# Reordering the hand-over from the forward to the inverse transform in a spectral filter beside a gated MLP

## The chip, the core and the metric

The kernel runs on one core of one Trainium2 chip. The metric is the device time of one execution in microseconds. The core has a matrix engine (TensorE, "PE" in the profile), a vector engine (VectorE, DVE), a scalar engine (ScalarE, ACT), a general engine (GpSimd, POOL) and SyncE (SP), which here only issues DMAs. Each engine works through its own queue in order; the engines meet through semaphores. DMAs are issued from the queues of SP, ACT and POOL.

## The reference

The input `x` is 2048 rows of 512 values in bf16. It is normalised by rows, and two branches are added to it:

```python
xn = layernorm(x)                                   # no scale, no shift
X  = rfft2(xn) * (w_r + 1j * w_i)                   # 2048 x 257 filter
A  = irfft2(X)
g, u = xn @ w_gate, xn @ w_up                       # 512 -> 1792
B  = (gelu(g) * u) @ w_down                         # 1792 -> 512
out = x + A + B
```

## The kernel before

The MLP branch is a steady stream of dense matrix products on TensorE. It goes over the rows in four blocks `b` of 512, and in each block over 14 slices `fc` of the hidden width: `gate(b, fc)` (four matmuls of line 851, a gelu on ScalarE in line 854), `up(b, fc)` (four matmuls of line 866, a multiply on VectorE in line 872), and between them pieces of the down projection (`down`, line 887, or `product`, seven matmuls of line 754).

The spectral branch is cut into small units that are slipped into this stream. The Fourier transforms are matrix products with tables of cosines and sines:

- Forward, in four chunks `m` of rows: `unit_D` (transform along the columns), then `units_A(m)`: two groups `g` of matmuls (lines 472 and 475), each copied out of its two PSUM banks by one instruction into the tile `tt` (line 480), and written to the DRAM scratch `scr1` by two DMAs `ri` of 128 KB (issued by the helper in line 337). `load_tv(m)` reads `scr1` back into the tile `tv`, in another arrangement, by two DMAs of 256 KB.
- Inverse, in eight groups `g`: `unit_B(g)` (matmuls of line 571 on `tv`, a copy in line 577, multiplies with the filter in line 582), `unit_C(g)` (line 596, with the twiddle table `cm`, a copy in line 601, a write to a second scratch), later `unit_E` (line 624) and `unit_F` (line 809). `unit_B(0)` needs all four chunks of `tv`.
- The last spectral column goes its own way in small steps `mini(0)` to `mini(4)`.

The filter comes from DRAM in eight slices, `load_W(s)`: eight DMAs of 64 KB each, four for `w_r` on POOL's queue and four for `w_i` on SP's. Slice `s` is what `unit_B(s)` multiplies with; `keep_256(s)` copies its last column aside on POOL (line 560). The table `cm` comes in four pieces of 192 KB on POOL's queue, each for two of the `unit_C`. Loads of this kind go through `load_late` (line 340), which makes the issue wait for the TensorE instruction that was last put into the program.

The order is written out by hand. After each gate, each up and each product the builder calls `hook()`, which counts up by one and puts into the program whatever `at(h, ...)` has planned for that number:

```python
for s, h0 in enumerate((20, 27, 34, 40, 61, 66, 70, 75)):
    for i, t in enumerate(load_W(s)):
        at(h0 + i // 2, t)
    at(89 + s // 2 if s > 3 else 47 + s, (keep_256, s))
```

`units_A(3)` stands at hook 44, `load_tv(3)` at 47, `unit_B(0)` at 59, `unit_B(1)`, `unit_C(0)` and `mini(1)` at 63, `unit_B(2)` and `unit_C(1)` at 68, `unit_B(3)` at 72, `unit_B(4)` at 77. The hooks 57, 60 and 63 follow a gate, 58, 61 and 64 an up, 59, 62 and 65 a product. PSUM has eight banks; `take(n, ...)` picks the bank, or the pair of banks, which by the planner's own reckoning of time is free first, and the semaphores then hold a matmul until its bank has really been emptied.

Of the kernel before, what the change touches and what calls it, by code (L numbers as in the profile page):

```python
# [7 lines left out]
ACT = mybir.ActivationFunctionType  # L8
ALU = mybir.AluOpType
BF16 = mybir.dt.bfloat16  # L10
F16 = mybir.dt.float16
# [4 lines left out]
KD = 256  # L16
# [8 lines left out]
SC_A = 2.0 ** -3  # L25
# [106 lines left out]
class _Prog:  # L132
# [17 lines left out]
    def op(self, eng, fn, r=(), w=(), dma=False, after=()):  # L150
        deps = [(ev, True) for ev in after]
        for k in r:
            if k in self.writer:
                deps.append((self.writer[k], True))
        for k in w:
            if k in self.writer:
                deps.append((self.writer[k], False))
            for ev in self.readers.get(k, ()):
                deps.append((ev, False))
        need = {}  # L160
        for (st, val), raw in deps:
            if st == eng and not dma and (eng == "pe" or not raw):
                continue
            need[st] = max(need.get(st, 0), val)
        known = self.known[eng]
        need = {s: v for s, v in need.items() if known.get(s, 0) < v}
        need = {s: v for s, v in need.items()
                if not any(s2 != s and self.clk[(s2, v2)].get(s, 0) >= v for s2, v2 in need.items())}
        for s, v in need.items():
            for a, b in self.clk[(s, v)].items():  # L170
                if known.get(a, 0) < b:
                    known[a] = b
        if dma:

            st = None if eng == "pool" else next((d for d in self.dsem if known.get(d, 0) >= self.cnt[d]), None)
            if st is None:
                st = "d%d" % (len(self.sem) - 4)
                self.sem[st] = self.es.enter_context(self.nc.semaphore("s_" + st))
                self.cnt[st] = 0
                if eng != "pool":  # L180
                    self.dsem.append(st)
            self.cnt[st] += 16
            ev, inc = (st, self.cnt[st]), 16
            clk = dict(known)
        else:
            self.cnt[eng] += 1
            ev, inc = (eng, self.cnt[eng]), 1
            clk = dict(self.lastclk[eng])
            for a, b in known.items():
                if clk.get(a, 0) < b:  # L190
                    clk[a] = b
        clk[ev[0]] = ev[1]
        self.clk[ev] = clk
        if not dma:
            self.lastclk[eng] = clk
        self.q[eng].append((fn, list(need.items()), ev[0], inc))
        for k in r:
            self.readers.setdefault(k, []).append(ev)
        for k in w:
            self.writer[k] = ev  # L200
            self.readers[k] = []
        return ev
# [12 lines left out]
def bass_parallel_sum__spectral_gfnet__glu_gated_geglu__prompt_kernel(  # L215
# [15 lines left out]
    c_cm = nc.inline_tensor(CM_np, name="c_cm")  # L231
    c_g = nc.inline_tensor(G_np, name="c_g")
    c_mm = nc.inline_tensor(MM_np, name="c_mm")
    scr1 = nc.dram_tensor("scr1", (64, 64 * KD), F16).ap()
    scr2 = nc.dram_tensor("scr2", (P, 32 * KD), BF16).ap()

    xv = A_x.rearrange("o (q b j) d -> b q (o j) d", b=2, j=NJ)
# [5 lines left out]
    with ExitStack() as es:  # L243
# [4 lines left out]
        op = pr.op  # L248
# [29 lines left out]
        tt = [early[:, 4096 + 1024 * i:5120 + 1024 * i].rearrange("p (b jj c) -> p b jj c", b=2, jj=2) for i in range(4)]  # L278
# [32 lines left out]
        def bank(i):  # L311
            return psum[:, i * 512:(i + 1) * 512]
# [4 lines left out]
        def pair(i):  # L317
            return psum[:, i * 512:(i + 2) * 512]
# [5 lines left out]
        def take(n, dur, hold=None, ops=1):  # L324
            i = min(range(9 - n), key=lambda i: max(free[i:i + n]))
            pt[0] += dur
            if hold is None:
                act_t[0] = max(act_t[0], pt[0] + 0.25) + 0.2 + 0.43 * n
                end = act_t[0]
            else:  # L330
                end = pt[0] + hold
            for k in range(i, i + n):
                free[k] = end
            return i

        def dma(eng, dst, src, r=(), w=()):
            return op(eng, lambda e: e.dma_start(dst, src), r=r, w=w, dma=True)  # L337
# [122 lines left out]
        def units_A(m):  # L460

            for g in range(2):
                bk = take(2, 0.5)
                i = (2 * m + g) % 4

                def fn(e, bk=bk, g=g):
                    ins = None
                    for jj in range(2):
                        j = 4 * m + 2 * g + jj
                        x4 = xs[j % 8]  # L470
                        for b in range(2):
                            e.matmul(bank(bk + b)[:, 256 * jj:256 * jj + 256], am[64 * b:64 * b + 64, j, 64:192], x4[64 * b:64 * b + 64, 0:256],
                                     start=True, stop=False, skip_group_check=True)
                        for b in range(2):
                            ins = e.matmul(bank(bk + b)[:, 256 * jj + 1:256 * jj + 256], am[64 * b:64 * b + 64, j, 0:128], x4[64 * b:64 * b + 64, 256:511],  # L475
                                           start=False, stop=True, skip_group_check=True)
                    return ins

                op("pe", fn, r=["am"] + [("xs", (4 * m + 2 * g + jj) % 8) for jj in range(2)], w=[("ps", bk), ("ps", bk + 1)])
                op("act", lambda e, bk=bk, i=i: e.activation(tt[i].rearrange("p b jj c -> p (b jj c)"), pair(bk), ACT.Copy, scale=SC_A),  # L480
                   r=[("ps", bk), ("ps", bk + 1)], w=[("tt", i)])
                n = 2 * m + g
                for ri in range(2):
                    dma("act" if m == 3 and ri else "sp", scr1[8 * n:8 * n + 8, :].rearrange("(l i) (x c) -> i x l c", i=2, c=KD)[ri],
                        tt[i][64 * ri:64 * ri + 64].rearrange("p b jj c -> p (b jj) c"), r=[("tt", i)], w=[("scr1", n, ri)])

        MA, TA, MB, MC, TC, ME = (mm[:, 0:256], mm[:, 256:320], mm[:, 320:384], mm[:, 384:640], mm[:, 640:704], mm[:, 704:768])
# [61 lines left out]
        def load_W(s):  # L549
            hs = slice(2 * s, 2 * s + 2)  # L550
            for k, src in enumerate((A_w_r, A_w_i)):
                v = src.rearrange("(k2 r c h) k -> c k2 r h k", r=2, c=2, h=16)
                for c in range(2):
                    for i in range(2):
                        p0 = 64 * c + 32 * i
                        yield (load_late, W[k][s % 4][p0:p0 + 32, :, :, 0:KW], v[c][:, :, hs, :], [("W", k, s, c, i)], [("Wf", s % 4, k, c, i)], "sp" if k else "pool")
# [349 lines left out]
        def at(h, *calls):  # L906
            plan.setdefault(int(h), []).extend(calls)
# [14 lines left out]
            at(10 + 2 * i, (load_late, wd_sb[:, f0:f1, :], wdv[:, f0:f1, :], [("wd", fc) for fc in range(f0, f1)]))  # L922
        at(18, (load_late, be[:], c_be.ap(), ["be"]))
        at(19, (load_late, mm[:], c_mm.ap(), ["mm"]))
        for s, h0 in enumerate((20, 27, 34, 40, 61, 66, 70, 75)):
            for i, t in enumerate(load_W(s)):
                at(h0 + i // 2, t)
            at(89 + s // 2 if s > 3 else 47 + s, (keep_256, s))
        cmv = c_cm.ap().rearrange("p (h r c) -> p h r c", h=NJ, r=2)
        for i, h0 in enumerate((45, 57, 63, 68)):  # L930
            hs = slice(4 * i, 4 * i + 4)
            at(h0, (load_late, cm[:, hs], cmv[:, hs], [("cm", 2 * i), ("cm", 2 * i + 1)], (["ev1"], ["ev1", ("xn", 0)], [("xn", 1), ("xn", 2)], [("xn", 2), ("xn", 3)])[i]))
        at(60, (load_late, gm[:], c_g.ap().rearrange("p (a c) -> p a c", a=4), ["gm"]))
# [14 lines left out]
        for m in range(4):  # L948
            h = (11, 22, 31, 39)[m]
            for i in range(4):  # L950
                at(h + i + (i if m < 1 else 0), (unit_D, 4 * m + i))
            at(h + 5 + (4 if m < 1 else 0), (units_A, m))
            if m == 3:
                at(h + 7, (mini, 0))
            at(h + 8 + (4 if m < 1 else 0), (load_tv, m))
        for g in range(9):
            h = int(59 + 4.6 * g)
            if g < 8:
                at(h, (unit_B, g))
            if g > 0:  # L960
                at(h, (unit_C, g - 1))
            if g == 1:
                at(h, (mini, 1))
            if g == 8:
                at(h - 2, (mini, 4))
                at(h, (mini, 2))
# [133 lines left out]
```

## Time and profile before

| | |
|---|---|
| five executions, us | 183.84, 184.87, 186.32, 186.37, 192.29; median 186.32 |
| the profiled execution | 184.87 us, span from first to last instruction 183.1 us |
| granted TensorE clock | 1.00 throughout |
| busy: TensorE, VectorE, ScalarE, GpSimd | 174.6, 130.6, 94.3, 53.5 us |
| DMA | 26.83 MB, 147 GB/s on average |
| two copies of the last chunk (line 480) | begin at 62.04 and 63.89 us, 1.02 us each |
| `load_tv(3)` issued, `unit_B(0)` started | 69.91 us, 76.05 us |

Busy time says how full an engine is, not what its work waits for. The chain of waits follows the last instruction back to what released it, step by step; the list of waits says for each engine and line what ended its idle time. TensorE's ends are modelled, so that its starts are the surer numbers.

### The profile page before, as it was taken

The page shows a single profiled execution, that of the slowest core. Times are in us where ns is not written, and L with a number is a line of the kernel's source. Part 1 is how long each engine was busy: PE and PEld are TensorE (multiplying, and loading weights), DVE is VectorE, ACT ScalarE, POOL GpSimd, SP SyncE. Part 2 cuts the span into 40 slices and gives each one's busy share as a digit, 9 for nine tenths or more (in the row PEclk, how much of TensorE's full clock was granted, in tenths as well). Part 3 has the DMA queues.
Part 4 walks back from the last instruction along what each step waited for, and adds up shares of the span by engine and source line. Part 5 has one row for each costly group of instructions (what it writes and reads, how often), then busy time and mean ns, then how long its engine had stood idle before and what let it go on. Part 6 is the DMA issues. An engine that isn't in the chain of part 4 may idle for free.

```text
span 183.1 us, 3824 instructions
## 1 busy us (share of the span) xinstructions
PE 174.6 (95%) x1417; PEld 108.0 (59%) x1417; DVE 130.6 (71%) x322; ACT 94.3 (52%) x157; POOL 53.5 (29%) x106
## 2 busy tenths in 40 slices
PE   7599999999999999889999999999999999999992
PEld 2278655564645456446565656556676767666882
DVE  2486989999256369447786658788777868998552
ACT  1334547767566352452746656534858577642110
POOL 2110081825234220175644000001254435640000
PEclk9999999999999999999999999999999999999999
DMA  4999999698978997137765112176055666643104
GB/s 109 288 260 306 328 252 328 168 228 143 219 101 187 122 217 120 43 102 173 207 184 148 57 57 61 58 216 246 0 95 103 123 115 116 107 68 59 32 0 115
DMA packets 26899, 26.83 MB, mean 147 GB/s; under 512 B 2961, under 2 KB 23825, under 8 KB 26753
## 3 DMA queue, kind: packets, MB, share of 16 engines
q1 hardware_dynamic: 20448, 17.78, 40.2%
q0 software_dynamic: 4272, 7.24, 19.0%
q10 hardware_dynamic: 2160, 1.57, 3.3%
q8 instruction: 11, 0.18, 0.4%
q14 instruction: 8, 0.06, 0.1%
HBM read 18.19 MB, written 6.29 MB: 134 GB/s over the span
## 4 chain that ended last, share of the span: by engine, by line
PE 74%; DMA 10%; DVE 7%; ACT 2%; issue 2%; SPq 2%; POOL 1%; ACTq 0%; DVEq 0%
PE ps L866 20%; PE ps L851 20%; PE ps L754 19%; DMA wu<-in_B_w_up_dram 5%; DMA tv<-scr 3%; PE ps L887 3%; DVE st L381 3%; DMA scr<-early 3%; PE ps L624 2%; PE ps L809 2%; PE ps L596 2%; SPq L337 2%; DVE hT L872 1%; PE ps L571 1%; PE ps L403 1%
## 5 line engine op out<-in xcount | busy, mean ns | idle before, releaser
L851 PE MATMUL ps<-xnT,wg 128*128 128x512 f16 (+1 forms) x248 | 58.6, 359 | 0.7 <-DMA wg<-in_B_w_gate_dram 0.6
L866 PE MATMUL ps<-xnT,wu 128*128 128x512 f16 (+1 forms) x248 | 58.6, 359 | 0.5 <-DMA wu<-in_B_w_up_dram 0.5
L872 DVE TENSOR_TENSOR hT<-ps,gl 128x512 bf16<-128x512 f32 (+1 forms) x62 | 39.3, 635 | 20.9 <-PE ps L866 11.9
L854 ACT ACTIVATE gl<-ps 128x512 bf16<-128x512 f32 (+1 forms) x62 | 34.5, 557 | 34.6 <-PE ps L851 33.8
L866 PEld LDWEIGHTS ps<-xnT,wu 128*128 128x128 bf16 x248 | 23.3, 98 | 20.8 <-DMA wu<-in_B_w_up_dram 1.1
L851 PEld LDWEIGHTS ps<-xnT,wg 128*128 128x128 bf16 x248 | 22.8, 98 | 16.8 <-issue 1.4
L340 POOL DMA_DIRECT2D wring<-in_A_w_r_dram x32 | 18.5, 610 | 17.7 <-DVE early L582 7.6
L633 POOL COPY tv<-tv 1x128 bf16<-1x128 bf16 x16 | 5.2, 323 | 42.6 <-ACT tv L631 42.6
L835 POOL DMA_DIRECT2D x_sb<-tv x16 | 13.1, 866 | 2.8 <-DVE tv L828 2.5
L582 DVE TENSOR_TENSOR early<-early,wring 128x1024 bf16<-128x1024 f16 x16 | 10.3, 687 | 5.0 <-ACT early L577 5.0
L381 DVE BATCH_NORM_STATS2 st<-x_sb 128x6 f32<-128x512 bf16 x16 | 10.6, 680 | 4.0 <-DMA x_sb<-in_A_x_dram 4.0
L754 PE MATMUL ps<-wd,hT 128*128 128x256 bf16 x98 | 12.5, 273 | 0.0
L448 ACT ACTIVATE early<-ps 128x512 f16<-128x512 f32 x16 | 9.5, 595 | 5.4 <-PE ps L444 5.4
L631 ACT ACTIVATE tv<-ps 128x512 bf16<-128x512 f32 x16 | 9.5, 595 | 3.8 <-PE ps L624 3.8
L577 ACT ACTIVATE early<-ps 128x1024 f16<-128x1024 f32 x8 | 8.2, 1022 | 6.2 <-PE ps L571 6.2
L815 ACT ACTIVATE tv<-ps 128x512 bf16<-128x512 f32 x16 | 9.5, 595 | 3.5 <-PE ps L809 3.5
L776 ACT ACTIVATE ps<-ps 128x256 f32<-128x256 f32 x14 | 5.2, 370 | 11.8 <-PE ps L754 11.8
L389 POOL TENSOR_TENSOR rstd<-vpe,mhalf 128x4 f32<-128x4 f32 (+1 forms) x5 | 4.5, 901 | 22.9 <-DVE vpe L388 22.9
L754 PEld LDWEIGHTS ps<-wd,hT 128*128 128x128 bf16 x98 | 9.3, 98 | 2.3 <-issue 0.2
L754 PE MATMUL ps<-arena,xnT 128*128 128x256 f16 x84 | 10.5, 273 | 0.0
L651 DVE TENSOR_TENSOR x_sb<-ps,x_sb 128x256 bf16<-128x256 f32 (+1 forms) x16 | 7.2, 451 | 4.4 <-PE ps L887 2.7
L480 ACT ACTIVATE early<-ps 128x1024 f16<-128x1024 f32 x8 | 7.9, 1022 | 4.6 <-PE ps L475 3.8
(104 smaller groups left out, 242.0 us busy)
## 6 DMA issues: line engine op xcount, KB each, us to landing
wring<-in_A_w_r_dram POOLq DMA_DIRECT2D x32, 64.2 KB, 3.5
wring<-in_A_w_i_dram SPq DMA_DIRECT2D x32, 64.2 KB, 3.1
tv<-scr SPq DMA_DIRECT2D x8, 256.0 KB, 5.8
scr<-early SPq DMA_DIRECT2D x8, 256.0 KB, 2.2
wring<-scr SPq DMA_DIRECT2D x4, 512.0 KB, 6.6
x_sb<-tv POOLq DMA_DIRECT2D x16, 128.0 KB, 2.6
scr<-early SPq DMA_DIRECT2D x14, 128.0 KB, 3.9
out_dram<-x_sb SPq DMA_DIRECT2D x28, 64.0 KB, 2.1
```

The costliest lines, as they stand in the source:

```text
L340: op(eng, lambda e: e.dma_start(dst, src), w=list(keys) + list(also), dma=True, after=[("pe", pr.cnt["pe"])])
L381: op("dve", lambda e: e.bn_stats(st[:, j, :], x_sb[:, j, :]), r=[("x", j, 0), ("x", j, 1)], w=[("st", j)])
L448: op("act", lambda e: e.activation(x4.rearrange("p (a c r) -> p a c r", a=2, r=4), bank(bk).rearrange("p (a r c) -> p a c r", a=2, r=4), A ...
L582: op("dve", lambda e, k=k: e.tensor_tensor(pp[i][k], xc[i], W[k][g % 4][:, :, :, 0:256], ALU.mult), r=[("xc", i)] + [key for c in range(2) ...
L631: op("act", lambda e: e.activation(z, bank(bk).rearrange("p (a c) -> p a c", a=4), ACT.Copy, scale=SC_E), r=[("ps", bk)], w=[zk] + (TVK if ...
L754: ins = e.matmul(o, st_(f), mv(f), start=(f == 0 and step in (0, 5)), stop=(f == 6), skip_group_check=True)
L815: op("act", lambda e: e.activation(o2, bank(bk), ACT.Copy), r=[("ps", bk)], w=[ok] + (TVK if j < 2 else []))
L835: op("pool", lambda e: e.dma_start(x_sb[:, j, :], ys, accum_op=ALU.add), r=[yk + (0,), yk + (1,), ("x", j, 0), ("x", j, 1)] + acc(j), w=ac ...
L851: ins = e.matmul(bank(bg)[:, 0:n], wg_sb[:, dc, fc * P:(fc + 1) * P], xnT[:, dc, c0:c0 + n], start=(dc == 0), stop=(dc == 3))
L854: op("act", lambda e: e.activation(gl[k % 3][:, 0:n], bank(bg)[:, 0:n], ACT.Gelu_apprx_tanh), r=[("ps", bg)], w=[("gl", k % 3)])
L866: ins = e.matmul(bank(bu)[:, 0:n], wu_sb[:, dc, fc * P:(fc + 1) * P], xnT[:, dc, c0:c0 + n], start=(dc == 0), stop=(dc == 3))
L872: op("dve", lambda e: e.tensor_tensor(hT[b % 2][:, fc, h0:h0 + n], bank(bu)[:, 0:n], gl[k % 3][:, 0:n], ALU.mult), r=[("ps", bu), ("gl", k ...
```

## The change

Five edits, all around the hand-over from the forward to the inverse transform:

1. The scratch `scr1` gets rows of 65 x 256 instead of 64 x 256 elements of 2 bytes; only the first 64 x 256 are written and read.
2. In the last chunk (`m == 3`) the copy of the second group goes to VectorE, as a multiply by the same constant; that of the first group stays on ScalarE.
3. In the last chunk one write of the second group is still issued from ScalarE's queue; that of the first group goes back to SP's.
4. The fourth filter slice is loaded from hook 53 instead of 40, its `keep_256` moves from hook 50 to 58, and the first piece of `cm` is loaded at hook 54 instead of 45.
5. `unit_C(0)` moves from hook 63 to 64, and `mini(1)` from 63 to 65.

```diff
-    scr1 = nc.dram_tensor("scr1", (64, 64 * KD), F16).ap()
+    scr1 = nc.dram_tensor("scr1", (64, 65 * KD), F16).ap()
...
-                op("act", lambda e, bk=bk, i=i: e.activation(tt[i].rearrange("p b jj c -> p (b jj c)"), pair(bk), ACT.Copy, scale=SC_A),
-                   r=[("ps", bk), ("ps", bk + 1)], w=[("tt", i)])
+                src, dst = pair(bk), tt[i].rearrange("p b jj c -> p (b jj c)")
+                late_one = m == 3 and g == 1
+                if late_one:
+                    op("dve", lambda e, dst=dst, src=src: e.tensor_scalar(dst, src, SC_A, None, ALU.mult), r=[("ps", bk), ("ps", bk + 1)], w=[("tt", i)])
+                else:
+                    op("act", lambda e, dst=dst, src=src: e.activation(dst, src, ACT.Copy, scale=SC_A), r=[("ps", bk), ("ps", bk + 1)], w=[("tt", i)])
                 n = 2 * m + g
                 for ri in range(2):
-                    dma("act" if m == 3 and ri else "sp", scr1[8 * n:8 * n + 8, :].rearrange("(l i) (x c) -> i x l c", i=2, c=KD)[ri],
+                    dma("act" if late_one and ri else "sp", scr1[8 * n:8 * n + 8, 0:64 * KD].rearrange("(l i) (x c) -> i x l c", i=2, c=KD)[ri],
                         tt[i][64 * ri:64 * ri + 64].rearrange("p b jj c -> p (b jj) c"), r=[("tt", i)], w=[("scr1", n, ri)])
...
-        for s, h0 in enumerate((20, 27, 34, 40, 61, 66, 70, 75)):
+        for s, h0 in enumerate((20, 27, 34, 53, 61, 66, 70, 75)):
             for i, t in enumerate(load_W(s)):
                 at(h0 + i // 2, t)
-            at(89 + s // 2 if s > 3 else 47 + s, (keep_256, s))
+            at(89 + s // 2 if s > 3 else (47, 48, 49, 58)[s], (keep_256, s))
...
-        for i, h0 in enumerate((45, 57, 63, 68)):
+        for i, h0 in enumerate((54, 57, 63, 68)):
...
             if g > 0:
-                at(h, (unit_C, g - 1))
+                at(h + (g == 1), (unit_C, g - 1))
             if g == 1:
-                at(h, (mini, 1))
+                at(h + 2, (mini, 1))
```

## The prediction

> **What bounds the kernel now.** I read the page's chain first, then TensorE's waits, the chain in order of time around them, and last the queues that feed that stretch.
>
> ```profile
> PE 74%; DMA 10%; DVE 7%; ACT 2%; issue 2%; SPq 2%; POOL 1%; ACTq 0%; DVEq 0%
> PE ps L571 <- DMA tv<-scr: 0.7, 1, 0.7
> PE ps L596 <- ACT gl L854: 0.4, 1, 0.4
> PE ps L514 <- ACT early L577: 0.2, 1, 0.2
> ```
>
> The chain is three quarters TensorE. Its list of waits holds, behind the start (33 us), only the last three lines: one wait for the scratch read into `tv` (first inverse unit, line 571), one for a gelu (line 596), one for a copy (line 514). Everything that this change can win on TensorE stands in these lines. The busy table by stretches says the same: TensorE is busy all the time from 33 to 168 us except in two stretches of 4 us:
>
> ```profile
> 72.00:76.00 4.00, 3.34 (x23) 1.98 (x21) 2.95 (x8) 0.96 (x2) 0.55 (x1) 1.00 0.50 86
> 80.00:84.00 4.00, 3.37 (x43) 1.95 (x36) 1.46 (x4) 2.40 (x3) 1.79 (x4) 1.00 0.66 172
> ```
>
> The second number is TensorE's busy time: 0.66 and 0.63 us idle, 1.29 together. The chain in order of time (start, duration) shows what leads to the first gap:
>
> ```profile
> 62.04 1.03 ACT early L480
> 63.10 0.67 ACTq L337
> 63.89 1.03 ACT early L480
> 64.94 4.88 DMA scr<-early
> 70.26 5.66 DMA tv<-scr
> 76.05 0.41 PE ps L571 x8
> ```
>
> Two copies of the last chunk run one behind the other on ScalarE, with a DMA issue of 0.67 us between them; then the scratch is written, read back, and TensorE, free at 75.35 (its product began at 74.42 and took 0.93), starts at 76.05. SP's and GpSimd's queues show what else was in flight:
>
> ```profile
> 59.00 2.63 SPq L340 DMA_DIRECT2D wring<-in_A_w_i_dram  x4
> 63.09 2.45 SPq L337 DMA_DIRECT2D scr<-early  x2
> 68.10 0.19 POOL L560 COPY w<-wring 128x4 bf16<-128x4 bf16 x1 [1.10 <-DMA wring<-in_A_w_i_dram]
> ```
>
> The fourth filter slice is issued just ahead of the scratch writes and has landed only when the GpSimd copy runs at 68.10. So the writes share the DMA engines with it (DMA share 0.90 from 56 to 64 us and 0.85 from 64 to 70).
>
> The second gap, in TensorE's order of time:
>
> ```profile
> 78.90 1.03 PE L851 MATMUL ps<-xnT,wg 128*128 128x512 f16 x4
> 79.85 0.41 PE L571 MATMUL ps<-tv,be 64*64 64x256 f16 x8
> 80.70 0.63 PE L596 MATMUL ps<-early,cmx 64*64 64x256 bf16 x16 [0.44 <-ACT gl L854]
> 81.52 0.20 PE L514 MATMUL ps<-mt,mm 64*64 64x16 f16 x4 [0.19 <-ACT early L577]
> 81.66 1.04 PE L866 MATMUL ps<-xnT,wu 128*128 128x512 f16 x4
> ```
>
> Between a gate and its up sit B(1), C(0) and mini(1). Replaying the planner's bank choice of the kernel before: C(0) gets the bank that this very gate has just filled, and mini(1) the pair of B(1). Each waits until ScalarE has emptied it.
>
> **The change, part by part.**
>
> *Second copy of the last chunk to VectorE, one write to SP.* The ACTIVATE of 1.02 us leaves ScalarE. No row shows this copy on VectorE. The nearest are the 512-wide and 256-wide multiplies out of PSUM of line 872, 688 and 417 ns: 1.06 ns an element, so 0.69 + 512 x 1.06 = 1.23 us for 1024. The other end is line 413's copy of 1024 f16 elements out of PSUM, 0.68 us; I take 1.23, because the source is f32. VectorE is idle there (2.75 us before its add at 63.45), so the copy runs from 62.4 to 63.65 instead of 63.89 to 64.92. The add behind it slips 0.2 us; nobody on TensorE waits for it. SP now issues three writes, at 63.09, 63.70 and 64.31 (0.61 each), ScalarE one at 63.70. The last issue moves from 64.94 to 64.31, 0.63 us earlier, at either duration of the copy, since SP's issues set it. ScalarE's gelu behind them moves from 65.63 to about 64.3; TensorE did not wait for it.
>
> *Fourth filter slice from hook 40 to 53.* Four GpSimd issues (2.33 us) and four SP issues (2.63 us) go out in front of the writes; 514 KB no longer share the rings with them. In the old positions they were done by 61.6 and held no queue up, so the gain is in the rings. The writes then took 4.88 us; those of the chunk before took 2.5 in the median. In the new place GpSimd issues its half from 70.3 and SP from 72.0, behind the `tv` read on SP. They land 3 to 7 us later (the medians of the lighter and the busiest stretch), by 81 at worst; the multiply that needs them belongs to B(3), at 90. Cover: 9 us. The two small copies of hook 58 wait on GpSimd for this landing, up to 81; queued behind them are `gm` (first needed at 127), the fifth slice (issued 78.9 before, then up to 2 us later, needed near 95) and the third twiddles (C(4), near 100). All covered. If that cover were gone, VectorE would stand at the multiply and each us would reach TensorE.
>
> *First twiddles from hook 45 to 54.* One GpSimd issue (0.57 us, 192 KB), at 72.4 instead of 63.7, landing 2.6 to 4.7 us later: 77.7 at the latest. C(0) needs them at about 79.8. Cover: 2 us; cost nothing.
>
> *Padded rows.* The same bytes and the same number of runs; only the pitch goes from 32,768 to 33,280 bytes. The trace first: the last `tv` read, 0.52 MB, moves its data between 70.75 and 73.3 us, then some 2.6 us pass until it counts as landed. Here the Trainium skill is weighed, since it speaks against this part. "DMA: Bandwidth & Descriptors", section "Latency and other measured facts", has pitches at large powers of two slowing copies, but from 512 KiB up, with 4 KiB of padding curing it and 192 B not. And "SBUF — State Buffer", section "Door 1: The DMA port swizzle", gives a destination of 16 partitions 4 of 16 ports, some 109 GB/s. Each half of the read goes to 16 partitions, the two halves to different ports: 262 KB / 109 = 2.4 us, an estimate from that page, and just what the trace shows (2.5). By that rule the ports set the read and padding is worth 0; were it aliasing in HBM, a part of 2.5 us could go. I take 0. Both leave the sum as it is, as the next step shows; in the other direction the bound is a read that doubles (rival 3).
>
> *What becomes of B(0)'s wait.* From the last write issue to B(0)'s turn there are now 75.35 - 64.31 = 11.04 us. Before, write and read took 75.92 - 64.94 = 10.98. So the wait goes even if nothing in the rings becomes faster, by a hair; with writes of 2.5 us it goes with 2.4 us to spare. Gain: 0.70.
>
> *C(0) and mini(1) one and two hooks later.* Gate, B(1), up, C(0), product, mini(1), gate. I worked the planner's choice on by hand: the same banks as before, C(0) still the gate's bank, but now 0.87 us later, when the gelu (0.60) is done; mini(1) still B(1)'s pair, after up, C(0) and the product, when the copy (1.02) is done. From hook 68 on all choices are the old ones. Price by rows: a B before a dense group costs 0.34 (76.05 to 76.39), a C 0.54 (86.13 to 86.67), a mini 0.14 (81.52 to 81.66): 1.02 in all, against 81.66 - 79.85 = 1.81. Gain 0.79; by the idle counter 0.63.
>
> *Sum.* 0.70 + 0.79 = 1.49 by starts, 1.29 by idle counters; I take **1.4**. TensorE is full behind it to 168 us, and the inverse stages are released by TensorE's own work, so all of it reaches the end: 184.87 (the profiled execution: span 183.1 and 1.77 around it) - 1.4 = 183.5. That execution lies 1.45 us under the median of 186.32. What makes the others longer is not shown. If it is late DMA, it sits where DMA ends the chain: 8.62 us at the start and 10.54 in this stretch, 55% here. An estimate: 0.8 us of the median's excess are further waiting of B(0), and go too. 186.32 - 1.4 - 0.8 = **184.1**, 1.2% below. A measurement of this kernel can tell about 1% from no change.
>
> **The rivals.**
>
> 1. *Both waits go, and nothing more* or half of it comes back: the filter slice and twiddles, from 70.3 on, now overlap the end of the `tv` read. For: the third chunk's read, beside filter loads, took 7.1 us, not 5.0 to 5.7. Against: the read should be issued by 68.5 and have its data by 72. Gain 0.4 to 1.4: 184.9 to 185.9.
>
> 2. *The filter slice is too late* and VectorE, in order, stands at B(3)'s multiply. Decides only past 89 us; landing was never above 8.3 us after issue, which gives 83. I give this almost nothing.
>
> 3. *Slower: the new pitch slows the scratch.* Rows no longer start on 32 KB; if write and read each doubled from their uncrowded 2.5 and 5.7 us, they would take 16.4, end at 80.7, and B(0) would wait 5.4 us. Less the 0.79 and the old 0.70: +3.9, 190.2. It decides past 11.04 + 1.49 = 12.5 us from last issue to landing. Against: run lengths stay 512 B and 16 KB, and every pitch stays a multiple of 512 B.
>
> **How the numbers follow.** Forecast (waits gone, with the further waiting of slower executions): 0.57, of it 0.44 above 1% gain and 0.13 below. Rival 1: 0.23, all within 1%. Rivals 2 and 3, or another new wait on this order: 0.20, of it 0.18 above 1% loss. Faster 0.44, same 0.38, slower 0.18. The range: the lowest execution before less the smaller gain, 183.84 - 1.29, gives 182.6; at the top it holds all of rival 1 and of the slower cases those up to 0.7 us above the old median, 187.0. The forecast's own range is 182.6 to 185.3.
>
> **What would show it.** Line 571 no longer waits for `tv`; lines 596 and 514 no longer wait for ScalarE; a VectorE row of about 1.23 us out of PSUM; last write issue near 64.3; `tv` issued by 68.5 and landed by 74; L560's wait for the filter slice near 77. The prediction is wrong if B(0) still waits, if a line of VectorE shows a wait for `wring`, or if TensorE has a new gap between 84 and 168.

## The result, and the profile after

The changed kernel takes 184.23 us in the median of 30 executions, the kernel before 185.61 us in the median of 51. Some executions of either kernel are slower, most of them at a lower granted clock (189.40 us at 0.982, for one), and the ratio is taken over the others: 0.9943, with a 95% interval of 0.9926 to 0.9960, which is 0.57%, or 1.06 us (0.74 to 1.37). That is inside the 1% that the prediction called no change.

The profiled execution of the changed kernel has a span of 182.5 us at a granted clock of 1.000, against 183.1. Line numbers behind the edit are up to four higher: the waits of lines 571, 596 and 514 are those of 575, 600 and 518 now. First the page's chain by engine:

```profile
PE 76%; DMA 11%; DVE 8%; issue 2%; SPq 2%; POOL 1%; ACT 0%; DVEq 0%
```

and TensorE's list of waits:

```profile
PE ps L575 <- DMA tv<-scr: 0.3, 1, 0.3
```

Of the three waits of before, one is left at half its length (0.34 us in the timeline), and those for ScalarE are gone. ScalarE has left the chain (2% before). The busy table by stretches (the second number is TensorE's busy time, the last but one the DMA share):

```profile
64.00:68.00 4.00, 4.00 (x26) 2.03 (x25) 3.52 (x9) 1.20 (x2) 0.00 (x0) 1.00 0.52 133
72.00:76.00 4.00, 3.71 (x25) 2.15 (x22) 3.03 (x8) 1.08 (x3) 1.88 (x4) 1.00 0.76 103
80.00:84.00 4.00, 4.00 (x45) 1.99 (x38) 2.32 (x5) 2.69 (x4) 3.10 (x6) 1.00 0.76 192
100.00:168.00 68.00, 68.00 (x577) 43.03 (x570) 53.25 (x147) 40.40 (x69) 18.07 (x33) 1.00 0.45 99
```

TensorE is idle for 0.29 us from 72 to 76 us (0.66 before) and not at all from 80 to 84 (0.63 before). Up to 168 us no new gap has come. The chain in order of time through the same stretch:

```profile
64.78 4.64 DMA scr<-early
...
69.90 6.01 DMA tv<-scr
...
76.05 0.41 PE ps L575 x8
```

Here is the surprise. The filter slice is gone from in front of the writes, but the last write still takes 4.64 us from issue to landing (4.88 before), and the read takes 6.01 (5.66 before). `unit_B(0)` starts at 76.05 us in both profiles; the forward matmuls of the last chunk had started 0.36 us later here (61.75 against 61.39), which lies in the start of the kernel.

The load of the 16 DMA engines shows what the moved slice did and did not do. First before, then after, from 62 to 78 us; each digit is 0.4 us, the busy share in tenths, and a packet is booked where it begins:

```profile
DMA  6585899999999997300000909996000008710000
DMA  0000000878889100000009699960296979999991
```

Before, the engines are busy until about 68.8 us. After, they are idle until about 64.8, then 0.7 to 0.9 busy with the four writes, and all but empty from 67.6 on. Yet the last write landed at 69.42. These are the packets that begin between 67.3 and 69.5 us:

```profile
q8 instruction: 1, 0.02, 2.7%
q1 hardware_dynamic: 17, 0.01, 2.5%
```

One packet of 16 KB of the queue that the profile names "instruction", which is none of the kernel's own DMAs, ran from 67.32 to 68.28 us. Sixteen packets of 512 B of the last write came only behind it, from 68.26 to 68.97. The trace has sixteen reports of landing for one write: fifteen were in by 67.61, 2.83 us after the issue, and the sixteenth at 69.42. So moving the slice did shorten the writes, in fifteen parts of sixteen; one part was held up.

The second gap, in TensorE's order of time:

```profile
78.89 1.03 PE L855 MATMUL ps<-xnT,wg 128*128 128x512 f16 x4
79.85 0.41 PE L575 MATMUL ps<-tv,be 64*64 64x256 f16 x8
80.19 1.04 PE L870 MATMUL ps<-xnT,wu 128*128 128x512 f16 x4
81.16 0.63 PE L600 MATMUL ps<-early,cmx 64*64 64x256 bf16 x16
81.72 0.94 PE L758 MATMUL ps<-arena 128*128 128x256 f16 x7
82.59 0.20 PE L518 MATMUL ps<-mt,mm 64*64 64x16 f16 x4
82.73 1.04 PE L855 MATMUL ps<-xnT,wg 128*128 128x512 f16 x4
```

From `unit_B(1)` to the next gate it takes 2.88 us by starts, where it took 3.45 (79.85 to 83.30): 0.57 us won.

Since the start of the kernel moves from execution to execution, I compare profiles from here on by TensorE's own starts, counted from the first forward matmul of the last chunk ("from F"). To the gate behind `mini(1)` it took 21.91 us before and takes 20.98 now: 0.93 won, 0.36 at `unit_B(0)` and 0.57 at the second gap. Where it did not wait, `unit_B(0)` at its old hook started 13.88 us from F; here it started at 14.30, and before at 14.66.

### The profile page after: what moved, and what is told of

It is laid out like the page before. It is cut to its first block, busy times and chain, and to the rows that moved or that the text cites. A ratio compares the mean times of both kernels' runs of the same rounds, so it can differ in the third digit from the quotient of the medians.

```text
span 182.5 us, 3825 instructions
## 1 busy us (share of the span) xinstructions
PE 175.7 (96%) x1417; PEld 108.3 (59%) x1417; DVE 131.8 (72%) x323; ACT 93.4 (51%) x156; POOL 53.4 (29%) x106
## 4 chain that ended last, share of the span: by engine, by line
PE 76%; DMA 11%; DVE 8%; issue 2%; SPq 2%; POOL 1%; ACT 0%; DVEq 0%
PE ps L855 20%; PE ps L870 20%; PE ps L758 19%; DMA wu<-in_B_w_up_dram 5%; PE ps L891 3%; DMA tv<-scr 3%; DVE st L381 3%; DMA scr<-early 3%; PE ps L600 2%; PE ps L813 2%; PE ps L628 2%; SPq L337 2%; PE ps L575 2%; DVE hT L876 1%; PE ps L403 1%
## 5 line engine op out<-in xcount | busy, mean ns | idle before, releaser
L581 ACT ACTIVATE early<-ps 128x1024 f16<-128x1024 f32 x8 | 8.2, 1023 | 5.8 <-PE ps L575 5.8
L758 PEld LDWEIGHTS ps<-arena,xnT 128*128 128x128 f16 x84 | 8.2, 98 | 2.2
L605 ACT ACTIVATE early<-ps 128x1024 bf16<-128x1024 f32 x8 | 8.2, 1020 | 2.0 <-PE ps L600 2.0
```

Of the source, the lines that this page charges most:

```text
L758: ins = e.matmul(o, st_(f), mv(f), start=(f == 0 and step in (0, 5)), stop=(f == 6), skip_group_check=True)
```

## The experiments

Four kernels take one part of the change each, one leaves a part out, four alter it, one joins what helped, and two repeat a kernel for a second profile. All in one table, in us; "tv issued" and "gate" (the one behind `mini(1)`) are counted from F. In "write queues" stand the last chunk's writes issued from SP and from ScalarE.

| kernel | filter slice | write queues | tv issued | wait of B(0) | gate | ratio to before |
|---|---|---|---|---|---|---|
| before; again | in front | 2 SP, 2 ScalarE | 8.52; 8.18 | 0.70; 0.70 | 21.91; 21.90 | 1 |
| hooks only | in front | 2, 2 | 9.42 | 2.03 | 22.66 | 1.0065 (1.0004 to 1.0126) |
| padding only | in front | 2, 2 | 9.19 | 1.55 | 22.76 | 0.9984 (0.9930 to 1.0039) |
| copy only | in front | 3, 1 | 8.66 | 1.25 | 22.45 | 1.0039 (0.9990 to 1.0089) |
| loads only | behind | 2, 2 | 7.43 | none | 21.13 | 0.9983 (0.9902 to 1.0064) |
| changed; again | behind | 3, 1 | 7.80; 7.80 | 0.34; 0.41 | 20.98; 21.05 | 0.9943; 0.9931 |
| changed, old pitch | behind | 3, 1 | 7.79 | 0.50 | 21.14 | 0.9931 (0.9898 to 0.9964) |
| changed, filter later | further behind | 3, 1 | 7.81 | 0.41 | 21.05 | 0.9919 (0.9880 to 0.9959) |
| changed, B(0) later | behind | 3, 1 | 7.66 | none | 20.57 | 0.9920 (0.9885 to 0.9955) |
| changed, two issues | behind | 2, 2 | 6.83 | none | 20.56 | 0.9898 (0.9852 to 0.9944) |
| two issues, mini | behind | 2, 2 | 7.54 | 0.17 | 20.59 | 0.9891 (0.9836 to 0.9945) |
| all three | behind | 2, 2 | 7.15 | none | 20.35 | 0.9895 (0.9848 to 0.9942) |

The profiles of "loads only" and "all three" have a mean granted clock of 0.991, and that of "changed; again" 0.989; in the stretch that the table is about, their gates and ups still take the usual 0.86 us. The ratios of the lower rows overlap with that of the change: what sets these kernels apart is the stretch, mostly in one profile each.

One more table takes the last write apart, from its issue on (from the times at which its sixteen parts landed):

| kernels | fifteen parts in | all in | tv issued from F |
|---|---|---|---|
| slice in front (5 profiles) | 4.1 to 5.4 | 4.55 to 5.77 | 8.18 to 9.42 |
| slice behind, 3 on SP (5) | 2.8 to 2.9 | 4.51 to 4.66 | 7.66 to 7.81 |
| slice behind, 2 and 2 (4) | 2.8 to 3.2 | 3.80 to 5.05 | 6.83 to 7.54 |

In each of the nine profiles with the slice behind, the sixteenth part came 1.0 to 1.9 us after the others, one 16 KB packet of the instruction queue ran while the write was in flight, and the write's last packets ended 0.4 to 0.9 us behind that packet. In the chunk before, where the changed kernel's profile has no such packet beside the writes, the last part of each of the four was at most 0.33 us behind. The trace does not tell which of the 16 engines a packet is on, and no run moved this packet; that it held the sixteenth part up is read from the order in time.

**Hooks only.**

```diff
-                at(h, (unit_C, g - 1))
+                at(h + (g == 1), (unit_C, g - 1))
             if g == 1:
-                at(h, (mini, 1))
+                at(h + 2, (mini, 1))
```

> The kernel before with edit 5 alone (unit_C(0) at hook 64, mini(1) at 65). Theory: the two waits for ScalarE (lines 596 and 514) go, and two further changes from dense to small matmuls cost 0.11 us each, so the distance from B(1)'s start to the next gate's start falls from 3.45 to 2.88 us, a gain of 0.57 us, ratio 0.997. Rival, the prediction's price: 0.79 us, distance 2.66 us, ratio 0.996. The wait of B(0) for tv stays near 0.7 us by both.

From `unit_B(1)` to the gate it took 2.88 us, as the theory said, not 2.66. But the wait of `unit_B(0)` before it, which theory and rival had near 0.7, was 2.03 us, as TensorE's waits and the chain show:

```profile
PE ps L571 <- DMA tv<-scr: 2.0, 1, 2.0
```

```profile
64.58 5.77 DMA scr<-early
...
70.78 6.08 DMA tv<-scr
```

Up to `unit_B(0)` this kernel's order is that of before, so the write leg of 5.77 us is not this edit's work. The time came out above that of before, by an interval that only just leaves out 1. In this profile the longer wait outweighs what the hooks won (the gate stands at 22.66, not 21.91); whether the other executions had it too is open.

**Copy only**: edits 2 and 3 in the kernel before.

> The kernel before with edits 2 and 3 alone (second copy of the last chunk on VectorE, one write back on SP's queue). Theory: only the issue moves; last write issue about 0.5 us earlier against TensorE's own clock, and B(0)'s wait falls by as much, from 0.70 to about 0.2 us, ratio 0.997. Rival (the rings are the limit, the issue does not matter while the filter slice is in them): the writes land at the same time, the wait stays at 0.7 us, ratio 1.000.

The last write was issued 0.53 us earlier from F than before (3.02 against 3.55), but needed 5.51 us to land, and the wait was 1.25 us:

```profile
64.51 5.51 DMA scr<-early
```

With the filter slice in front, an earlier issue did not show: nearer to the rival, though one profile is weak, since this leg spreads.

**Loads only**: edit 4 in the kernel before.

> The kernel before with edit 4 alone (fourth filter slice, first twiddles and one keep_256 moved behind the scratch). Theory: the write chain falls little, from 4.9 to about 4.6 us, and the tv read gets longer, from 5.7 to about 6.0 us, because the slice is now issued into it: B(0)'s wait stays at 0.6 to 0.8 us, ratio 1.000. Rival, the prediction's view: the writes take 2.5 us, the wait goes, 0.70 us gained, ratio 0.996.

`tv` was issued 7.43 us from F, earlier than in the whole change (7.80), and `unit_B(0)` did not wait, starting 13.88 us from F. The theory fell. The rival had the effect but not its size:

```profile
69.21 0.64 ACTq L337 DMA_DIRECT2D scr<-early  x1
73.08 0.77 SPq L337 DMA_DIRECT2D tv<-scr  x2
78.67 0.93 PE L754 MATMUL ps<-arena,xnT 128*128 128x256 f16 x7
79.53 0.41 PE L571 MATMUL ps<-tv,be 64*64 64x256 f16 x8
```

The last write was issued at 69.21 us and had landed at 73.01, so the write leg was 3.8 us and not 2.5. This kernel issues its last write latest of all with the slice behind (3.56 us from F) and reads earlier than the whole change: its sixteenth part was 1.0 us behind the others, not 1.8. The time itself is too uncertain to tell 0.4% from nothing.

**Padding only**, and **the changed kernel with the old pitch**:

```diff
-    scr1 = nc.dram_tensor("scr1", (64, 64 * KD), F16).ap()
+    scr1 = nc.dram_tensor("scr1", (64, 65 * KD), F16).ap()
...
```

> The kernel before with edit 1 alone (rows of the scratch 33,280 bytes apart). Theory, as predicted: the tv reads keep their durations (5.0 to 7.1 us over the four chunks) and the wait of B(0) stays at 0.7 us, ratio 1.000. Rival a: padding spreads the runs, the last read falls by 1 us or more, the wait goes, ratio 0.996. Rival b: the pitch slows the scratch, the read grows by 1 us or more, ratio 1.005.

> The changed kernel with the old pitch (edit 1 undone). Theory: the pitch sets nothing; write leg 3.9 to 4.7 us, last tv read 5.2 to 6.1 us as in the changed kernel, B(0)'s wait 0 to 0.5 us, ratio to the kernel before 0.994. Rival: the padding is what keeps the read short beside the filter loads; without it write and read together grow by 1 us or more, B(0)'s wait is above 1.3 us, ratio 0.999.

Alone, the padding came with a write leg of 5.53 us and a read of 5.84, both inside what the kernels with the slice in front and no padding had. The read was as the theory said; the wait of 1.55 us, for which it had 0.7, was not, and it comes from the write leg. Taken out of the change, the padding left both legs as they were; the chain of that kernel:

```profile
64.48 4.64 DMA scr<-early
69.60 6.18 DMA tv<-scr
```

The write leg is 4.64 us again, and the read 6.18 against 6.01. The pitch sets neither leg here.

**The filter slice later still.**

```diff
-        for s, h0 in enumerate((20, 27, 34, 53, 61, 66, 70, 75)):
+        for s, h0 in enumerate((20, 27, 34, 60, 61, 66, 70, 75)):
```

(and its `keep_256` from hook 58 to 65)

> The changed kernel with the fourth filter slice from hook 60 instead of 53 (its keep_256 at 65), so that it is issued only when tv has been read. Theory: the slice was what made the last tv read 6.0 us; alone it takes 5.0 us or less, B(0) does not wait, ratio 0.993; the slice still lands 5 us ahead of B(3)'s multiply, at which VectorE does not wait. Rival: the read's length is its own (ports and completion), it stays at 5.7 to 6.1 us and the wait at 0.3 us, ratio 0.994.

```profile
65.83 4.66 DMA scr<-early
70.96 6.08 DMA tv<-scr
```

The read stays at 6.08 us with no filter load beside it. The rival was right in the number: the slice did not make it long. One load of 192 KB for `cm` is still issued beside it (at 72.94 us), and no run took that away.

**Both ScalarE issues again** (edit 3 undone, the copy still on VectorE).

```diff
-                    dma("act" if late_one and ri else "sp", scr1...
+                    dma("act" if m == 3 and ri else "sp", scr1...
```

> The changed kernel with edit 3 undone: both ri=1 writes of the last chunk from ScalarE's queue again, the copy still on VectorE. Theory: the four issues now go out two by two, the last at about 2.4 us behind the first forward matmul instead of 3.0, so tv is issued 0.6 us earlier against TensorE and B(0)'s wait of 0.34 us goes; ratio 0.993. Rival: landing is set by the slowest write and not by the issue, the leg from last issue to landing grows by the same 0.6 us, the wait stays near 0.3 us; ratio 0.994.

SP's queue in this kernel, with two writes where the changed kernel has three, and with the read behind them:

```profile
63.21 1.28 SPq L337 DMA_DIRECT2D scr<-early  x2
68.34 0.77 SPq L337 DMA_DIRECT2D tv<-scr  x2
```

The read goes out 6.83 us from F instead of 7.80 (7.54 and 7.15 in the two later kernels with the same issues), and the wait is gone; the gate stands at 20.56. The read is 0.97 us earlier, more than the 0.6 of the theory, and only part of this is the issue: fifteen parts of the last write were in 5.6 us from F in all three of these kernels, against 5.9 in the changed one, 0.3 us earlier. The rest, and the spread from 6.83 to 7.54, is the sixteenth part. ScalarE pays nothing for the second issue: its gelu started 3.31 us from F, and 3.09 in the changed kernel, and no one waited.

**B(0) one hook later.**

```diff
-                at(h, (unit_B, g))
+                at(h + (g == 0), (unit_B, g))
```

> The changed kernel with unit_B(0) at hook 60 instead of 59, behind one more gate. Theory: tv has then landed (the gate gives 0.86 us, the wait was 0.34), B(0) does not wait, and as it now stands between a gate and an up the dense and small matmuls change as often as before; gain 0.3 us on the changed kernel, ratio 0.992. Rival: what is won at B(0) is lost at once, since C(0) at hook 64 then waits for B(0)'s multiply on VectorE or mini(1) for a bank; ratio 0.994 or above.

As the theory said: no wait, and 20.57 us to the gate. Two ways to take the wait away give the same place, 0.41 and 0.42 us ahead of the change, so that wait was the whole of what was left there.

**Two issues, and mini(1) directly behind C(0).**

```diff
-                at(h + 2, (mini, 1))
+                at(h + 1, (mini, 1))
```

> The changed kernel with edit 3 undone and mini(1) at hook 64, directly behind unit_C(0). Theory: each change from dense to small matmuls costs 0.11 us, and one of them goes: the distance from B(1)'s start to the next gate's start falls from 2.88 to 2.77 us, B(0) does not wait, ratio 0.989. Rival: mini(1) now comes before ScalarE has emptied B(1)'s pair of banks (it has about 0.1 us to spare), waits 0.1 us or more, and the distance stays at 2.88 us or grows; ratio 0.990 or above.

```profile
79.64 0.41 PE L575 MATMUL ps<-tv,be 64*64 64x256 f16 x8
79.98 1.04 PE L870 MATMUL ps<-xnT,wu 128*128 128x512 f16 x4
80.95 0.63 PE L600 MATMUL ps<-early,cmx 64*64 64x256 bf16 x16
81.41 0.18 PE L518 MATMUL ps<-mt,mm 64*64 64x16 f16 x4
81.52 0.94 PE L758 MATMUL ps<-arena 128*128 128x256 f16 x7
82.30 1.03 PE L855 MATMUL ps<-xnT,wg 128*128 128x512 f16 x4
```

2.66 us, not 2.77: the small group of four matmuls, set alone between two dense groups, had cost 0.22 us, twice what I had put down. C, mini and product now take 0.46, 0.11 and 0.78 us; in the changed kernel they took 0.56, 0.14 and 0.87. Part of this was given back here by a write leg of 5.05 us, which left a wait of 0.17 us.

**The changed kernel and the kernel before, profiled again.**

> The changed kernel once more, on the chip of the run beside it, for a second profile. Theory: write leg 4.6 us, last tv read 6.0 us, B(0)'s wait 0.3 to 0.5 us, ratio 0.994, 0.3 to 0.5% above the kernel with edit 3 undone. Rival: what the kernel with edit 3 undone gained lay in the chip that it ran on; both have the same ratio here.

> The kernel before once more, for a second profile of its wait. Theory: the wait of B(0) in the first profile (0.70 us) was a short one; typical is 1.2 to 2.0 us, as in the two kernels with the same forward part (hooks alone 2.03, padding alone 1.55), with a write leg near 5.5 us instead of 4.88. Rival: 0.7 us is typical, and the two others were long.

The changed kernel again had the write leg of 4.64 us. Its ratio, 0.9931 (0.9897 to 0.9965), stood beside 0.9891 of "two issues, mini" on the same chip; the intervals overlap, so the times alone do not separate the two. The kernel before waited 0.70 us once more, with a write leg of 4.55 us: the theory that its first wait was a short one fell.

**All three together.**

> The changed kernel with three edits together: edit 3 undone, mini(1) at hook 64 behind unit_C(0), unit_B(0) at hook 60. Theory: what each gave adds up as far as it is not the same wait: B(0) waits in no execution (0.34 us, given by either of two edits) and mini(1) saves 0.22 us, so from the first forward matmul of the last chunk to the gate behind mini(1) it takes 20.98 - 0.34 - 0.22 = 20.4 us, with 21.9 before; ratio 0.989 to 0.990. Rival: with B(0) later, C(0)'s multiply or a bank is late and mini(1) or C(0) waits; 20.6 us or more, ratio 0.991 or above.

20.35 us from F, no wait, and 0.9895 (0.9848 to 0.9942). `tv` had landed 13.43 us from F, so that `unit_B(0)` would not have waited at its old hook either. It is the shortest stretch of all, 1.56 us shorter than before and 0.63 shorter than the change. It beats the kernel before; that it beats the changed kernel is shown by the stretch, not by the times, whose intervals meet.

## Why the prediction was right, and where it was not

The measured 184.23 us lies by the predicted 184.1 and in the range, but partly by luck: the forecast was 2.2 us below a median of 186.32, and the median over more executions is 185.61. The gain itself is 1.06 us, half of the forecast. It falls within 1%, which had 0.38, not above it, which had 0.44; and it lies in the band of rival 1 (0.4 to 1.4): half of one wait came back, but the slice, to which rival 1 put it down, was not the reason ("filter later"). One of the prediction's own signs of being wrong came true: `unit_B(0)` still waits. `tv` was issued at 69.55 us and not by 68.5, and landed at 75.91 and not by 74. The other two signs, a wait for `wring` and a new gap, did not come.

- **VectorE's copy**: 1.23 us forecast, 1.23 measured.

```profile
62.84 1.23 DVE L483 TENSOR_SCALAR early<-ps 128x1024 f16<-128x1024 f32 x1 [1.79 <-PE ps L475]
```

- **The last issue**: 0.63 us earlier forecast, 0.52 measured from F (3.03 against 3.55), since SP's three issues took 0.65 each. Edit 3, which the sum had passed over as no cost, has one: with VectorE doing the copy, ScalarE stood idle from 63.42 to 64.10 us, and SP's third issue became the last. With that write given back to ScalarE the wait was gone in two profiles and half gone in a third; fifteen parts of the last write came 0.3 us earlier by it, and what the read gained beyond or short of that lies in the sixteenth.
- **B(0)'s wait, 0.70 us**: 0.36 won. The step that failed is the write leg of 2.5 us "with 2.4 us to spare". The size was right for fifteen parts of the last write (2.83 us) and wrong for its landing (4.64), which the sixteenth part sets; the four writes of the chunk before, from which the 2.5 came, had no part so late (their last one took 2.41). An estimate from these numbers: had the sixteenth part come with the others, `tv` would have landed near 74.1 us, 1.6 ahead of `unit_B(0)`'s turn at 75.71. The same step's other reckoning, "by a hair" with no faster rings, left 0.06 us, but only up to the landing at 75.92; TensorE started 0.13 us later, so a wait of 0.07 was left in the sum. The last issue came 0.11 us later than forecast, and write and read took 0.15 us longer together (11.13 against 10.98): to rounding, the 0.34 measured.
- **Filter slice**: its new place was covered, as forecast; VectorE shows no wait for `wring`, and the GpSimd copies ran at 79.07 us. What the old place cost was not a steady amount: fifteen parts of the last write took 4.1 to 5.4 us there, and 2.8 to 3.2 with the slice behind. The prediction charged the median's excess, 0.8 us, to such waiting. The two profiles of the kernel before gave 0.70 both times, and the two kernels of the same forward order ("padding only", "hooks only") 1.55 and 2.03. So the waiting does vary; that it made the median of before is not shown, and the measured 1.06 us has little room for it beside the 0.93 of the two profiles.
- **Padding at 0**: right, by both experiments, but the reading of the trace beside it was not. The row from which the prediction took 2.5 us for the data of the `tv` read books a packet where it begins. By the packets' own ends the data moved from 70.86 to 75.05 us, 4.2 us, at 125 GB/s for both halves together, and landed 0.9 us later; over the fourteen profiles it took 3.9 to 4.4 us. So the trace does not bear out the estimate of 2.4 us from the ports, and what sets the read stays open.
- **C(0) and mini(1), 0.79 us**: 0.57 measured. The banks and the waits were as forecast. The mis-sized term is the row of 0.14 us for a mini: that row was of a mini that followed another small group. Alone between product and gate it cost 0.22 more. Put behind C(0), the stretch took 2.66 us, which is the prediction's own sum.
- **Rivals**: nothing of 2 or 3 was seen.

## What to carry to other kernels

When a chain of copy, write and read back ends in a wait, count it from the event that starts it, and ask of its last DMA not only when most of it has landed but when the last of its parts has. A median over other DMAs does not tell that. An earlier last issue helps by what it is earlier (0.3 us here in fifteen parts), and a queue that is idle just then can give it. A small group of matmuls has its price where it stands: put it beside another small one. And a short wait at one point can be taken away by moving the waiter one slot, as surely as by making its data earlier.

## What the runs showed of the hardware that I had not expected

With the filter slice moved away, fifteen of the sixteen parts of the last 128 KB write to DRAM were in after 2.8 to 3.2 us, and the sixteenth after 3.8 to 5.05. Each time a 16 KB packet of the instruction queue (0.9 to 1.4 us long) ran while the write was in flight, and the write's last packets ended behind it. As far as the trace tells, a packet that none of the kernel's DMAs asked for decided when the write counted as landed; no run tested that. The read of two times 256 KB back took 5.66 to 6.18 us with filter loads beside it or none, and whatever the pitch. And four matmuls of 0.2 us, alone between two dense groups, cost TensorE 0.22 us more than beside another small group.
